# A new order for an mLSTM layer with a ReLU block: attention inputs first, all four decay blocks on TensorE

## The chip, the cores and the metric

One core of a Trainium2 chip. The metric is the device time of one execution in microseconds; the profile shows one execution, its span and what each engine did in it. Engines are named as in the profile: PE is TensorE (PEld its weight loads), DVE is VectorE, ACT is ScalarE, POOL is GpSimd, SP issues most transfers. A line such as L547 is a line of the kernel.

## The reference

Two stages. First a recurrent attention with exponential gates over 768 steps, for 4 batches of 8 heads of 40 elements; then a normalisation and a two-layer ReLU block (320 to 1280 to 320) on the result, added to it.

```python
m_new = np.maximum(f_gate[:, :, t] + m, i_gate[:, :, t])
f_stab = np.exp(f_gate[:, :, t] + m - m_new)
i_stab = np.exp(i_gate[:, :, t] - m_new)
C = f_stab[:, :, None, None] * C + i_stab[:, :, None, None] * np.einsum('bhd,bhe->bhde', vt, kt)
n = f_stab[:, :, None] * n + i_stab[:, :, None] * kt
h_tilde = np.einsum('bhde,bhe->bhd', C, qt)
y[:, :, t] = o * h_tilde / np.maximum(np.abs(np.einsum('bhd,bhd->bh', n, qt)[:, :, None]), 1.0)

xn = (x - mu) / np.sqrt(var + 1e-06) * g_ln
out = x + np.maximum(xn @ w_ch1, 0.0) @ w_ch2
```

All inputs are float32. The two weight matrices come as float64 bit patterns and are turned into float32 on the chip.

## The kernel before

The 768 steps are cut into 6 chunks of 128; a chunk and a batch make one of 24 **steps** (st = 4 * chunk + batch), and two steps a **pair** p of 256 rows for the ReLU block. Inside a chunk the recurrence is done as attention with a decay: a 128x128 block of weights per head, plus a carried state for all but the first chunk.

Each piece of work is a small function, and ORDER, a table of some 1180 words, calls them one after the other; `S.4@1@2` calls S for step 4 on PSUM banks 1 and 2. No scheduler changes the order: each engine's instructions run in the order of the table, and an engine that waits holds all that is behind it on its queue. SP's transfers and the few that ScalarE issues itself (gst, gse) stand in their engines' queues likewise. The framework gives each transfer one of eight completion counters in turn, over both queues; a transfer is issued only when the one that had its counter before has landed.

The pieces, with their lines:
- ld (L198) loads q and k of a step, tok (L203) the rows of k, v and the output gate of a pair, wl (L598) a raw weight block: block 0 is the rest of w_ch1, odd blocks are columns of w_ch1 (512 wide), even ones rows of w_ch2 (640 wide).
- gm, gg, gate, gu make the gate rows of a chunk (VectorE, from the second chunk on partly GpSimd); gst (L275) and gse (L283) write two of them to memory, from where G (L212) and eg (L223) read them back, broadcast over partitions. gta, gtr (L287) transpose gate columns, gca, gcr copy them, gr and gex are exponents.
- The decay block of a step: G loads it, sel (L320, GpSimd) masks it, ex (L331, ScalarE, 8 heads) takes the exponents. For steps below GP the block is made in PSUM instead by gx (L340, L346), ten matmuls, and ex reads it there.
- S (L363) multiplies k and q, P (L370, VectorE) applies the block, pv (L449) multiplies with v. km (L384, GpSimd) and kv (L415) update the state; qm (L376, GpSimd) and int (L400) read it. st (L434, ScalarE in the first chunk) stores the state, sig (L314, ScalarE) takes the output gate's tanh. n1, n2, n3 (VectorE) and nx, sq (ScalarE), np (GpSimd) normalise, T (L513, L514) transposes, xh and xl split the result into a high and a low part.
- m1 (L547) and hh, hl (L552, L559) are the first layer in column blocks f of 256, m2 (L574 to L576) the second, ob (L581) the sum, out (L588) the store.
- A weight block passes cA (L607, ScalarE), cB (L614, GpSimd), cT twice (L624, L628, VectorE), cH (L650, ScalarE, the high part) and cL (the low part: L679 on VectorE; for blocks 1 and 3 cI on TensorE and L676 on ScalarE). m1 and m2 need both parts, so each f waits for its blocks. cR copies part of block 0 to other partitions.
- fill (L726) are matmuls whose result nobody reads, 20 of them at the start.

Of the kernel before, what the change touches and what calls it, by code (L numbers as in the profile page):

```python
# [44 lines left out]
g0 ini id gin wl.2 wl.0 cst fill.513 fill.513 fill.496 fill.496 fill.496 fill.496 fill.256 fill.256 fill.256 fill.256  # L45
fill.320 fill.320 fill.320 fill.320 fill.257 fill.257 fill.257 fill.257 ld.1 ld.2 gm.0 wl.3 gg.0 ld.0 gate.0 gu.0
gst.0 gm.1 gg.1 cA.2 G.2 G.3 cB.2 gate.1 ld.3 gex.1 gst.1 tok.0 gx.1@0@1 cA.0 cB.0 tok.1 cT.2.0 wl.1 gse.1 ld.5 cT.2.1
gu.1 gta.0@2 gx.0@3@4 gr.0 gca.0 cT.0.0 ex.1.1 gtr.0@5 ex.1.0 S.1@2@6 g8 gm.2 ex.0.1 gta.1@1 fill.512 ld.4 gcr.0 P.1.1
gg.2 S.2@0@5 gr.1 cT.0.1 cA.3 gtr.1@4 fill.513 cH.2 cB.3 ex.0.0 fill.513 gca.1 P.1.0 cH.0 cT.3.0 S.0@1@6 cL.2 sel.2
fill.513 int.0@2@3 gcr.1 gate.2 P.0.0 gex.2 fill.513 gu.2 gst.2 P.0.1 ex.2.1 fill.512 fill.512 cT.3.1 gse.2 sel.3  # L50
gta.2@4 fill.512 ex.2.0 fill.512 gm.3 fill.512 S.3@1@6 cL.0 gg.3 ex.3.0 fill.513 cH.3 P.2.0 fill.512 cR.2 fill.512
gr.2 cR.0 P.2.1 cI.3@0 ex.3.1 eg.2 P.3.0 G.4 gca.2 gate.3 gtr.2@5 sig.0 km.1 pv.0 wl.4 P.3.1 cR.1 gst.3 gu.3 gcr.2
cL.3 int.1@4@5 pv.1 n1.0 gex.3 n2.0 gse.3 kv.1@1 km.0 gm.4 gta.3@6 n3.0 int.2@2@3 st.1 gg.4 kv.0@0 gr.3 n1.1 gtr.3@1
nx.0 gca.3 pv.2 n2.1 sq.0 gcr.3 n3.1 sig.1 int.3@4@5 pv.3 np.0 G.5 st.0 tok.2 cA.1 n1.2 T.0@6 km.3 wl.5 gate.4
fill.512 nx.1 fill.512 ld.6 n1.3 km.2 sq.1 n2.2 kv.3@1 cR.3 n2.3 ld.9 xh.0 T.1@0 cB.1 n3.2 gst.4 wl.9 kv.2@2 gex.4
n3.3 np.1 xh.1 S.5@3@4 nx.2 xl.1 gu.4 sq.2 fill.512 fill.512 nx.3 xl.0 fill.512 st.2 S.4@0@5 cT.1.0 sq.3 np.2 st.3
T.2@6 gm.5 gse.4 np.3 T.3@2 m1.0.1.0@1 xh.2 cT.1.1 xh.3 qm.5 xl.2 cH.1 wl.6 m1.0.1.1 xl.3 gta.4@6 gg.5 hh.0.1 gca.4
cI.1@2 gr.4 hl.0.1 gtr.4@6 m1.1.1.0@1 gcr.4 sel.4 cL.1 gate.5 gex.5 gst.5 int.5@6@7 cB.4 gse.5 m1.0.0.0@2 ex.4.0 sd.5
gu.5 m1.0.0.1 ex.4.1 P.4.0 m1.1.1.1 cA.4 sel.5 P.4.1 hh.0.0 cT.4.0 gta.5@0 m1.1.0.0@5 hh.1.1 qm.4 gca.5 ex.5.0 hl.0.0
m1.1.0.1 hl.1.1 ex.5.1 cT.4.1 m2.0.0.0@0 P.5.0 hh.1.0 wl.7 int.4@1@2 km.5 G.8 cH.4 P.5.1 pv.4 km.4 sig.2 hl.1.0 pv.5  # L60
sd.4 cL.4 m2.0.0.1@3 cA.5 cB.5 n1.5 n1.4 m2.1.0.1@4 cT.5.0 n2.5 m2.1.0.0@5 cT.5.1 m2.1.1.0 n2.4 cH.5 wl.8 n3.5 ld.7
m2.0.1.0 n3.4 nx.5 sq.5 cL.5 m2.1.1.1 nx.4 np.5 m2.0.1.1 sq.4 cB.9 cA.9 m1.1.2.0@6 np.4 cT.9.0 m1.1.2.1 cT.9.1
m1.0.2.0@7 cH.9 wl.10 cB.6 G.6 hh.1.2 ld.8 kv.4@1 cL.9 eg.3 cA.6 kv.5@2 m1.0.2.1 hl.1.2 tok.3 cA.7 cB.7 st.4 G.9
cT.6.0 m1.0.4.0@6 G.7 hh.0.2 G.11 st.5 ld.10 cT.6.1 m1.1.4.0@1 sel.8 hl.0.2 cH.6 m1.1.4.1 cT.7.0 ex.8.0 m1.0.4.1 cL.6
ex.8.1 cT.7.1 S.6@2@7 cB.8 cA.8 m2.0.2.1 cH.7 cT.8.0 m2.0.2.0 hh.0.4 cL.7 hh.1.4 m2.1.2.0 hl.0.4 m2.1.2.1 hl.1.4 cA.10
cB.10 cT.8.1 m1.0.3.0@6 cH.8 cT.10.0 m1.0.3.1 cL.8 sel.6 m1.1.3.0@1 hh.0.3 cT.10.1 ex.6.1 m1.1.3.1 hl.0.3 cH.10
m2.0.3.1 P.6.1 ex.6.0 cL.10 T.4@6 qm.7 T.5@7 m2.0.3.0 hh.1.3 P.6.0 xh.4 m2.0.4.1 hl.1.3 xh.5 qm.6 xl.4 m2.1.3.0 ob.0.1
m2.0.4.0 xl.5 out.0.1 sig.3 km.6 eg.4 m2.1.3.1 ob.0.0 km.7 ld.11 m1.2.0.0@2 out.0.0 tok.4 sel.9 m1.2.1.0@1 m1.2.0.1
ex.9.0 S.7@3@6 sel.7 ex.9.1 S.8@0@7 ex.7.0 m2.1.4.0 sel.11 P.8.0 hh.2.0 P.8.1 ex.7.1 m1.2.3.0@0 P.7.0 ex.11.1 m1.2.3.1
hl.2.0 ob.1.0 S.9@3@7 ex.11.0 P.7.1 m2.2.0.1@2 P.9.0 P.9.1 kv.7@5 kv.6@6 m1.2.4.0@3 m2.2.0.0@7 m2.1.4.1 m1.2.1.1  # L70
ob.1.1 hh.2.3 hl.2.3 m1.2.4.1 hh.2.1 km.9 sig.4 hl.2.1 m1.2.2.0@4 km.8 hh.2.4 m1.2.2.1 hl.2.4 m2.2.1.0 hh.2.2 hl.2.2
S.10@0@1 int.6@3@4 pv.6 sd.6 st.6 m2.2.1.1 n1.6 n2.6 m2.2.2.1 n3.6 m2.2.3.1 sq.6 nx.6 np.6 int.7@3@4 pv.7 sd.7 qm.8
st.7 m2.2.2.0 n1.7 n2.7 T.6@6 qm.9 n3.7 m2.2.3.0 xh.6 int.8@3@4 pv.8 xl.6 sq.7 kv.9@5 nx.7 sd.8 G.10 np.7 kv.8@6 n1.8
m2.2.4.0 ld.13 n2.8 tok.5 st.8 eg.5 n3.8 T.7@3 m2.2.4.1 xh.7 ob.2.0 sq.8 xl.7 S.11@4@6 out.2.0 nx.8 ld.15 np.8 ob.2.1
ld.12 m1.3.2.0@7 out.1.0 P.11.0 sel.10 G.13 P.11.1 m1.3.2.1 ex.10.0 m1.3.0.0@3 hh.3.2 P.10.0 T.8@2 m1.3.4.0@4 ex.10.1
hl.3.2 m1.3.0.1 xh.8 P.10.1 xl.8 m1.3.3.0@6 hh.3.0 sig.5 km.11 hl.3.0 m1.3.3.1 km.10 m1.3.1.0@0 hh.3.3 qm.11 hl.3.3
m1.3.1.1 m1.3.4.1 hh.3.1 hl.3.1 m2.3.0.0@7 m2.3.0.1@1 int.9@2@3 S.13@0@6 sd.9 qm.10 st.9 pv.9 m2.3.1.1 sel.13 ld.17
n1.9 eg.6 n2.9 m2.3.1.0 n3.9 ex.13.0 G.12 ld.14 m2.3.2.0 out.1.1 nx.9 P.13.0 out.2.1 m2.3.3.0 ex.13.1 T.9@5 sq.9
m2.3.2.1 P.13.1 xh.9 np.9 m2.3.3.1 xl.9 hh.3.4 int.11@2@3 hl.3.4 S.12@0@6 sd.11 qm.13 int.10@4@5 m2.3.4.1 sd.10 sel.12
# [5 lines left out]
xh.11 kv.13@2 ob.4.0 sq.12 S.15@3@5 st.12 out.4.0 nx.12 xl.11 np.12 G.16 S.16@1@4 G.15 tok.7 m2.4.3.1 out.3.0
m1.5.0.0@0 m1.5.0.1 m1.5.2.0@6 sel.16 hh.5.0 hl.5.0 m2.4.4.1 ex.16.0 m2.5.0.0@0 ob.4.1 sel.15 ex.16.1 P.16.0
m1.5.1.0@7 ex.15.0 P.16.1 m1.5.2.1 ex.15.1 m1.5.1.1 P.15.0 hh.5.2 m2.5.0.1@1 P.15.1 hh.5.1 km.15 hl.5.2 sig.7 T.12@4
km.14 m1.5.3.0@3 hl.5.1 xh.12 xl.12 m1.5.3.1 m2.5.1.0 hh.5.3 hl.5.3 m1.5.4.0@5 int.13@6@7 S.17@3@4 sd.13 qm.14 st.13
pv.13 kv.15@2 qm.15 n1.13 G.17 m1.5.4.1 n2.13 G.19 n3.13 m2.5.1.1 ld.19 hh.5.4 tok.8 nx.13 hl.5.4 m2.5.2.1 eg.8 sq.13
# [704 lines left out]
```

## Time and profile before

| | |
|---|---|
| median of 3 runs | 342.15 us (339.23 to 343.68) |
| the profiled execution | 344.09 us, its span 341.6 us |
| TensorE busy | 323.3 us (95%), 5182 matmuls |
| VectorE busy | 185.6 us (54%) |
| ScalarE busy | 156.7 us (46%) |
| GpSimd busy | 114.5 us (34%) |
| memory | 50.25 MB moved, mean 147 GB/s |

Busy time is the time in which an engine executes something; the shares are means over a start in which all engines and the transfers are in use at once, and a long later part in which TensorE is the only full one. A row of a timeline gives the start, the length, engine, line, what is written and read, the count, and in brackets how long the engine was idle before it and what released it.

### The profile page before, as it was taken

Reading aid. Unit: us, or ns where it says so; the run is one execution under the profiler, and the core shown is the slowest. Engines: PE = TensorE matmul, PEld = TensorE weight load, DVE = VectorE, ACT = ScalarE, POOL = GpSimd, SP = SyncE. Lnnn points to the kernel's source line nnn. Section 1 sums busy time; section 2 is a strip of 40 time slices with the busy share of each in tenths; the row PEclk is TensorE's granted clock in tenths of the full one; section 3 lists DMA queues with packets and bytes.
Section 4 is the critical chain, followed back from the end, with each engine's and each line's share of the span. In section 5 each row is a group of like instructions: output and inputs, shape, how many; then the busy total and the mean of one; then the engine's idle time right before and its main releaser. Section 6 shows DMA issues by size and latency. Waiting matters only on the chain.

```text
span 341.6 us, 11893 instructions
## 1 busy us (share of the span) xinstructions
PE 323.3 (95%) x5182; PEld 301.7 (88%) x5182; DVE 185.6 (54%) x429; ACT 156.7 (46%) x405; POOL 114.5 (34%) x163
## 2 busy tenths in 40 slices
...
GB/s 230 274 361 209 297 263 126 230 242 338 12 148 112 2 221 258 56 201 263 18 30 317 3 264 223 53 4 208 372 60 2 176 12 118 4 60 0 79 0 38
DMA packets 16287, 50.25 MB, mean 147 GB/s; under 512 B 2092, under 2 KB 5612, under 8 KB 16236
## 3 DMA queue, kind: packets, MB, share of 16 engines
...
q14 instruction: 11, 0.09, 0.1%
...
## 4 chain that ended last, share of the span: by engine, by line
PE 81%; DMA 14%; DVE 2%; ACT 1%; issue 1%; ACTq 1%; DVEq 0%
PE banks L547 30%; PE banks L574 11%; PE banks L576 10%; PE banks L575 10%; DMA qk<-in_qk_dram 10%; PE banks L363 5%; PE banks L449 5%; PE banks L400 3%; DMA gsc<-gc 2%; PE banks L415 2%; PE banks L513 2%; DMA w<-gsc 2%; PE banks L514 1%; DVE wt L628 1%; ACT w L331 1%
## 5 line engine op out<-in xcount | busy, mean ns | idle before, releaser
L575 PE MATMUL banks<-w2l,hh 128*128 128x320 f32 x240 | 74.7, 311 | 3.2 <-DVE w2l L679 2.9
L576 PE MATMUL banks<-w2h,hl 128*128 128x320 f32 x240 | 75.0, 313 | 2.9 <-DVE hl L559 2.9
L574 PE MATMUL banks<-w2h,hh 128*128 128x320 f32 x240 | 77.4, 322 | 0.0
L552 ACT ACTIVATE hh<-banks 128x512 fp32r<-128x512 f32 x60 | 35.0, 592 | 86.3 <-PE banks L547 73.5
L559 DVE SCALAR_TENSOR_TENSOR hl<-banks,hh 128x512 fp32r<-128x512 f32 x60 | 40.9, 688 | 61.5 <-ACT hh L552 61.4
L547 PE MATMUL banks<-xh,w1h 128*128 128x256 f32 x360 | 64.0, 286 | 0.7 <-DVE w L370 0.7
L547 PE MATMUL banks<-xh,w1l 128*128 128x256 f32 x360 | 62.3, 282 | 0.0
L331 ACT ACTIVATE w<-w,ar_sb 128x128 f32<-128x128 f32 x176 | 53.9, 389 | 16.2 <-POOL w L320 14.2
L547 PEld LDWEIGHTS banks<-xh,w1h 128*128 128x128 f32 x360 | 51.5, 188 | 1.9 <-DVE w L370 0.9
L547 PEld LDWEIGHTS banks<-xh,w1l 128*128 128x128 f32 x360 | 51.1, 188 | 0.0
L576 PEld LDWEIGHTS banks<-w2h,hl 128*128 128x128 f32 x240 | 45.7, 190 | 3.7 <-DVE hl L559 3.1
L547 PE MATMUL banks<-xl,w1h 128*128 128x256 f32 x240 | 48.0, 282 | 0.7 <-issue 0.7
L575 PEld LDWEIGHTS banks<-w2l,hh 128*128 128x128 f32 x240 | 45.8, 191 | 3.1 <-DVE w2l L679 3.1
L574 PEld LDWEIGHTS banks<-w2h,hh 128*128 128x128 f32 x240 | 45.8, 191 | 1.4 <-issue 0.7
L370 DVE TENSOR_TENSOR w<-banks,w 128x512 f32<-128x512 f32 x48 | 31.7, 684 | 17.0 <-ACT w L331 6.8
L376 POOL TENSOR_TENSOR qe<-qk,eg 104x512 f32<-104x512 f32 x20 | 27.4, 1378 | 35.3 <-PE banks L400 29.7
L547 PEld LDWEIGHTS banks<-xl,w1h 128*128 128x128 f32 x240 | 36.9, 188 | 0.8 <-issue 0.8
L501 POOL TENSOR_SCALAR rs<-rs 128x1 f32<-128x1 f32 x24 | 5.4, 227 | 87.9 <-ACT junk L495 87.8
L320 POOL TENSOR_SCALAR_AFFINE_SELECT w<-w 128x1024 f32<-128x1024 f32 x22 | 25.3, 1155 | 22.5 <-DMA w<-gsc 22.5
L384 POOL TENSOR_TENSOR kp<-tok,ar_sb 128x320 f32<-128x320 f32 x20 | 14.3, 731 | 38.5 <-PE banks L415 29.1
L581 DVE SCALAR_TENSOR_TENSOR y<-banks,rs,y 128x320 f32<-128x320 f32 x24 | 13.1, 550 | 26.0 <-PE banks L576 25.7
L363 PE MATMUL banks<-qk 40*64 40x128 f32 (+1 forms) x704 | 26.4, 275 | 0.0
...
## 6 DMA issues: line engine op xcount, KB each, us to landing
tok<-in_tok_dram SPq DMA_DIRECT2D x12, 968.0 KB
w<-gsc SPq DMA_DIRECT2D x22, 512.0 KB
...
wraw<-in_w1a_dram SPq DMA_DIRECT2D x5, 512.0 KB
...
```

The source lines that it names most:

```text
L320: nc.gpsimd.affine_select(out=w, in_=w, pattern=[[0, H], [1, C]], compare_op=ALU.is_ge, fill=NEG, base=0, channel_multiplier=-1)
L331: nc.scalar.activation(out=w[:, h], in_=ps[:, hh], func=AF.Exp, bias=ar_sb[:, c, 0, b * H + h:b * H + h + 1])
L363: nc.tensor.matmul(s_t[st, z][m, g], t[r, 1, g, m], t[r, 0, g], start=True, stop=True, skip_group_check=True)
L370: nc.vector.tensor_tensor(out=w, in0=s_t.pop((st, half)), in1=w, op=ALU.mult)
L376: nc.gpsimd.tensor_tensor(out=t, in0=qk_t[st][:, 0], in1=eg_t[p][:, j], op=ALU.mult)
L449: nc.tensor.matmul(Y[m, h], w[:, h, m], tok_t[p][:, j, h * VA:(h + 1) * VA], start=(c == 0), stop=(c == 0 or g == 3), skip_group_check=True,)
L547: nc.tensor.matmul(ps[:, i], a, x, start=(n == 0), stop=(n == len(ops) - 1))
L552: nc.scalar.activation(out=t, in_=h1_t[p, f], func=AF.Relu)
L559: nc.vector.scalar_tensor_tensor(out=l.rearrange("p a t -> p (a t)"), in0=ps.rearrange("p a t -> p (a t)"), scalar=0.0, in1=t.rearrange("p ...
L574: nc.tensor.matmul(ps, t[:, i, sl], w2h[:, ff], start=(ff == 0), stop=False)
L575: nc.tensor.matmul(ps, t[:, i, sl], w2l[:, ff], start=False, stop=False)
L576: nc.tensor.matmul(ps, l[:, i, sl], w2h[:, ff], start=False, stop=(ff == KF - 1))
```

## The change

ORDER is written anew, and GP goes from 2 to 4: the decay blocks of steps 2 and 3 are made by gx too. With that G.2, G.3, sel.2, sel.3 and gst.0 go, and gx.2 and gx.3 come; five float32 fills (fill.513) stand in the table instead of seven, the 13 fill.512 and the 16 others remain. All other pieces are the same ones in other places. km alternates its two buffers in the order of the calls, not by step. The variant "q" of CX that cA and cB now know isn't used, since CX is unchanged.

```diff
-GP = 2
+GP = 4
 NE = 4
 CX = "ppppppppppp"
@@ ORDER, its first words
-g0 ini id gin wl.2 wl.0 cst fill.513 fill.513 ...
+gin ini id g0 ld.0 ld.2 wl.0 fill.513 fill.513 ...
@@ km
+        kp_t[st] = kps[len(kp_t) % 2]
         kn = tok_t[p][:, j, VT:VT + DM].rearrange("p (h e) -> p h e", h=H)
         nc.gpsimd.tensor_tensor(
-            out=kps[st % 2][:, :DM].rearrange("p (h e) -> p h e", h=H), in0=kn,
+            out=kp_t[st][:, :DM].rearrange("p (h e) -> p h e", h=H), in0=kn,
@@ kv
-        kf = kps[st % 2]
+        kf = kp_t[st]
@@ cA
-        nc.scalar.activation(out=t.bitcast(F32), in_=hi.bitcast(F32), func=AF.Copy, scale=TINY)
+        if CX[n] == "q":
+            nc.gpsimd.tensor_scalar(out=t.bitcast(F32), in0=hi.bitcast(F32), scalar1=TINY, scalar2=None, op0=ALU.mult)
+        else:
+            nc.scalar.activation(out=t.bitcast(F32), in_=hi.bitcast(F32), func=AF.Copy, scale=TINY)
@@ cB
-        if CX[n] == "p":
+        if CX[n] in "pq":
```

The first twelve transfers on SP's queue, from the program's start, before (wraw is a raw weight block, qk the q and k of a step, w a broadcast gate row, tok a pair's rows):

```order
L187 DMA g0_sb_121<-in_gate0_dram 96x256
L191 DMA gin_122<-in_gates_dram 32x1280
L598 DMA wraw_155<-in_w2_dram 128x640
L598 DMA wraw_157<-in_w1r_dram 128x640
L194 DMA g_sb_104<-in_consts_dram 128x3
L198 DMA qk_178<-in_qk_dram 104x1024
L198 DMA qk_180<-in_qk_dram 104x1024
L598 DMA wraw_183<-in_w1a_dram 128x512
L198 DMA qk_189<-in_qk_dram 104x1024
L212 DMA w_202<-gsc_131 128x1024
L212 DMA w_204<-gsc_131 128x1024
L198 DMA qk_208<-in_qk_dram 104x1024
```

and now:

```order
L190 DMA gin_122<-in_gates_dram 32x1280
L186 DMA g0_sb_121<-in_gate0_dram 96x256
L197 DMA qk_155<-in_qk_dram 104x1024
L197 DMA qk_157<-in_qk_dram 104x1024
L598 DMA wraw_159<-in_w1r_dram 128x640
L193 DMA g_sb_104<-in_consts_dram 128x3
L598 DMA wraw_180<-in_w1a_dram 128x512
L197 DMA qk_182<-in_qk_dram 104x1024
L202 DMA tok_185<-in_tok_dram 128x1936
L598 DMA wraw_191<-in_w1a_dram 128x512
L202 DMA tok_194<-in_tok_dram 128x1936
L197 DMA qk_203<-in_qk_dram 104x1024
```

The q/k blocks of steps 0, 2 and 1, both tok blocks and the q/k block of step 3 have moved ahead, the first block of w_ch2 from the third place to the thirteenth, and the two w are gone.

ScalarE's first instructions, before (gsc and esc are the two written gate rows, w_214 and w_240 the decay blocks in PSUM, wt a weight block on its way):

```order
L275 DMA gsc_131<-gc0_127 32x128
L607 ACT_TABLE_LOAD
L607 ACTIVATE wt_200<-wraw_155 128x640
L279 ACTIVATE gg1_126<-gc1_128 32x128
L275 DMA gsc_131<-gc1_128 32x128
L607 ACTIVATE wt_225<-wraw_157 128x640
L283 DMA esc_132<-gg1_126 32x128
L309 ACTIVATE uu0_129<-uu0_129,gc0_127 96x128
L331 ACTIVATE w_214<-banks_99,ar_sb_110 128x128 x8
L331 ACTIVATE w_240<-banks_99,ar_sb_110 128x128 x4
L309 ACTIVATE uu1_130<-uu1_130,gc1_128 32x128
L607 ACTIVATE wt_299<-wraw_183 128x512
```

and now, behind the table load:

```order
L278 ACTIVATE gg1_126<-gc1_128 32x128
L308 ACTIVATE uu0_129<-uu0_129,gc0_127 96x128
L282 DMA esc_132<-gg1_126 32x128
L610 ACTIVATE wt_226<-wraw_159 128x640
L330 ACTIVATE w_207<-banks_99,ar_sb_110 128x128 x8
L330 ACTIVATE w_228<-banks_99,ar_sb_110 128x128 x4
L610 ACTIVATE wt_283<-wraw_180 128x512
L330 ACTIVATE w_228<-banks_99,ar_sb_110 128x128 x4
L330 ACTIVATE w_272<-banks_99,ar_sb_110 128x128 x4
L653 ACTIVATE w1h_111<-wt_226,g_sb_104 64x640 x2
L330 ACTIVATE w_309<-banks_99,ar_sb_110 128x128 x4
```

The exponents of four decay blocks follow each other, with the weight blocks 0 and 1 between them; the first gate row isn't written any more.

GpSimd at the two last weight blocks (w_ch2's, cB of blocks 8 and 10), before, with the decay selects, qm and km around them:

```order
L614 TENSOR_SCALAR wraw_970<-wraw_970 128x640
L614 TENSOR_SCALAR wraw_1043<-wraw_1043 128x640
L320 AFFINE_SELECT w_1046<-w_1046 128x1024
L376 TENSOR_TENSOR qe_1294<-qk_975,eg_1070 104x512
L376 TENSOR_TENSOR qe_1318<-qk_554,eg_1070 104x512
L384 TENSOR_TENSOR kp0_119<-tok_1101,ar_sb_110 128x320
L384 TENSOR_TENSOR kp1_120<-tok_1101,ar_sb_110 128x320
L320 AFFINE_SELECT w_1107<-w_1107 128x1024
L320 AFFINE_SELECT w_1118<-w_1118 128x1024
L320 AFFINE_SELECT w_1122<-w_1122 128x1024
```

and now:

```order
L617 TENSOR_SCALAR wraw_1077<-wraw_1077 128x640
L384 TENSOR_TENSOR kp0_119<-tok_1101,ar_sb_110 128x320
L384 TENSOR_TENSOR kp1_120<-tok_1101,ar_sb_110 128x320
L617 TENSOR_SCALAR wraw_1170<-wraw_1170 128x640
L384 TENSOR_TENSOR kp0_119<-tok_1190,ar_sb_110 128x320
L384 TENSOR_TENSOR kp1_120<-tok_1190,ar_sb_110 128x320
L375 TENSOR_TENSOR qe_1449<-qk_493,eg_1231 104x512
L375 TENSOR_TENSOR qe_1470<-qk_671,eg_1231 104x512
```

The selects have left this place, and the two qm stand behind the km of both pairs. VectorE at the same two blocks (wt_1186 and wt_1225 before, the low parts w2l; hl and P between them):

```order
L628 SCALAR_TENSOR_TENSOR wt_1186<-wraw_970,wt_1186 128x640
L624 SCALAR_TENSOR_TENSOR wt_1225<-wt_1225,wraw_1043 128x640
L679 SCALAR_TENSOR_TENSOR w2l_114<-wt_1186,w2h_113 128x640
L628 SCALAR_TENSOR_TENSOR wt_1225<-wraw_1043,wt_1225 128x640
L559 SCALAR_TENSOR_TENSOR hl_1274<-banks_99,hh_1259 128x512
L370 TENSOR_TENSOR w_1046<-banks_99,w_1046 128x512
L679 SCALAR_TENSOR_TENSOR w2l_114<-wt_1225,w2h_113 128x640
L370 TENSOR_TENSOR w_1046<-banks_99,w_1046 128x512
```

and now (wt_1301 and wt_1346):

```order
L682 SCALAR_TENSOR_TENSOR w2l_114<-wt_1188,w2h_113 128x640
L627 SCALAR_TENSOR_TENSOR wt_1301<-wt_1301,wraw_1077 128x640
L631 SCALAR_TENSOR_TENSOR wt_1301<-wraw_1077,wt_1301 128x640
L682 SCALAR_TENSOR_TENSOR w2l_114<-wt_1301,w2h_113 128x640
L559 SCALAR_TENSOR_TENSOR hl_1348<-banks_99,hh_1336 128x512
L627 SCALAR_TENSOR_TENSOR wt_1346<-wt_1346,wraw_1170 128x640
L559 SCALAR_TENSOR_TENSOR hl_1391<-banks_99,hh_1382 128x512
L631 SCALAR_TENSOR_TENSOR wt_1346<-wraw_1170,wt_1346 128x640
L682 SCALAR_TENSOR_TENSOR w2l_114<-wt_1346,w2h_113 128x640
```

Behind each cB on GpSimd the two cT and the low part follow on VectorE as before; both P have moved away from between them.

## Rows read from the trace of the kernel before

**Rows 1.** busy us by stretch: us, PE, PEld, DVE, ACT, POOL; clock, DMA share, GB/s

```profile
0.00:8.10 8.10, 6.38 (x20) 3.92 (x21) 3.39 (x15) 2.18 (x3) 4.20 (x18) 1.00 0.72 226
8.10:45.00 36.90, 31.49 (x408) 22.06 (x406) 26.21 (x66) 23.74 (x70) 24.06 (x38) 0.91 0.94 291
45.00:95.00 50.00, 43.00 (x554) 40.63 (x552) 40.84 (x66) 32.88 (x81) 29.20 (x32) 0.93 0.63 190
95.00:338.20 243.20, 242.40 (x4208) 235.13 (x4206) 114.58 (x282) 97.92 (x254) 57.01 (x77) 1.00 0.37 115
```

**Rows 2.** TensorE's waits, whole run (us in total, times, longest)

```profile
PE banks L575 <- DVE w2l L679: 2.9, 1, 2.9
PE banks L576 <- DVE hl L559: 2.9, 1, 2.9
PE banks L287 <- ACT uu L309: 2.2, 1, 2.2
PE banks L415 <- ACT w1l L676: 2.0, 1, 2.0
```

**Rows 3.** stretches after TensorE's waits, columns as in rows 1

```profile
33.80:37.00 3.20, 3.17 (x53) 2.95 (x55) 1.46 (x7) 3.20 (x9) 2.06 (x4) 0.50 0.82 230
92.00:94.70 2.70, 2.70 (x13) 2.70 (x12) 1.28 (x3) 2.48 (x7) 0.00 (x0) 0.50 0.01 3
```

**Rows 4.** ScalarE's timeline (start us, us), then two pieces of the chain of waits

```profile
25.24 0.72 ACT L314 ACTIVATE tok<-tok 128x640 f32<-128x640 f32 x1
29.85 0.31 ACTq L275 DMA_DIRECT2D gsc<-gc  x1
30.20 0.60 ACT L676 ACTIVATE w1l<-banks 128x512 fp32r<-128x512 f32 x1 [4.25 <-DVE y L471]
32.82 0.32 ACTq L283 DMA_DIRECT2D esc<-gg  x1
...
4.84 6.59 DMA gsc<-gc
16.14 16.30 DMA qk<-in_qk_dram
```

**Rows 5.** timeline of GpSimd, then of VectorE, around the last weight blocks

```profile
79.73 3.82 POOL L376 TENSOR_TENSOR qe<-qk,eg 104x512 f32<-104x512 f32 x2 [3.73 <-DMA eg<-esc]
83.50 1.41 POOL L384 TENSOR_TENSOR kp<-tok,ar_sb 128x320 f32<-128x320 f32 x2
84.86 3.77 POOL L320 TENSOR_SCALAR_AFFINE_SELECT w<-w 128x1024 f32<-128x1024 f32 x3
...
79.74 0.82 DVE L628 SCALAR_TENSOR_TENSOR wt<-wraw,wt 128x640 int32<-128x640 int32 x1
82.32 4.32 DVE L679 SCALAR_TENSOR_TENSOR w2l<-wt,w2h 128x640 fp32r<-128x640 f32 x1
86.56 2.75 DVE L628 SCALAR_TENSOR_TENSOR wt<-wraw,wt 128x640 int32<-128x640 int32 x1
```

**Rows 6.** two weight lines' VectorE instructions: ns least/median/most

```profile
L624 DVE SCALAR_TENSOR_TENSOR wt<-wt,wraw x11: 677/825/1923, 8.5 to 80.5; 128x640 int32<-128x640 int32 x6, 128x512 int32<-128x512 int32 x5
...
L679 DVE SCALAR_TENSOR_TENSOR w2l<-wt,w2h x5: 809/818/4316, 16.9 to 90.4; 128x640 fp32r<-128x640 f32 x5
```

**Rows 7.** TensorE's timeline: one decay block, four float32 fill matmuls

```profile
9.92 0.59 PE L340 MATMUL banks<-mk_bf,id_bf 128*128 128x512 bf16 x2
10.44 1.16 PE L346 MATMUL banks<-gc,id_sb 32*128 32x128 f32 x16
...
17.52 1.98 PE L726 MATMUL banks<-id_sb 128*128 128x512 f32 x4
```

**Rows 8.** ScalarE's exponents from PSUM until 45 us (xcount, busy us, mean ns)

```profile
L331 ACT ACTIVATE w<-banks,ar_sb 128x128 f32<-128x128 f32 x16 | 4.3, 385 | 0.3 <-DVE ar_sb L299 0.3
```

**Rows 9.** page, transfers issued: count, size of each

```profile
tok<-in_tok_dram SPq DMA_DIRECT2D x12, 968.0 KB
w<-gsc SPq DMA_DIRECT2D x22, 512.0 KB
```

149 lines of the change are left out of this document (74 added, 75 removed).

## The prediction

> **What bounds the kernel now.** I read the stretches first, then TensorE's waits, then the granted clock, then the queues behind the waits. By stretch [rows 1], TensorE is busy 242.4 of the 243.2 us from 95 to 338: there is nothing to win there except TensorE work itself. All that can be won lies before 95. From 8.1 to 45 (the first m1 starts at 45) it works 31.5 of 36.9 us, from 45 to 95 it works 43.0 of 50.0: 5.4 + 7.0 = 12.4 us idle. Four waits make 10.0 of the 12.4 [rows 2].
>
> Each pair of waits is followed by a stretch at the lower of the two clock levels (1.2 instead of 2.4 GHz): 0.50 from 33.8 to 37 and 0.50 from 92 to 94.7 [rows 3]; the timeline shows the same level from about 33.5 to 40.3 and from about 90 to 95. The first is full of small matmuls that lose less than half: I put it at 2.7 us. The second is about 4.9 us of wide matmuls, half of it lost: 2.4 us. So 12.4 + 2.7 + 2.4 = 17.5 us is the most that better feeding can give back.
>
> Why TensorE waits, first pair: ScalarE's queue is in order, and stands in front of two small transfers that it issues itself. After the tanh at 25.24 nothing starts until the gate row's transfer is let go at 29.85; the eviction of the low half of a weight block (w1l) follows at 30.20, and TensorE had waited 2.0 us for it. The next such transfer goes at 32.82, and 2.2 us of TensorE wait for the exponent behind it [rows 2, 4]. The chain of waits names what was late: a q/k transfer issued at 16.14 that landed 16.30 us later, behind all that was already queued; and SP's own queue stood 6.59 us, from 4.84 to 11.43, before its ninth transfer [rows 4].
>
> Second pair: VectorE is 100% busy from 80 to 90, but with two instructions stretched. The low half of a weight block (w2l) takes 4.32 us, the next weight step (L628) 2.75, while GpSimd runs instruction after instruction until 88.6 [rows 5]. Undisturbed the first takes 0.81 at the least [rows 6], and the second took 0.82 at 79.74 [rows 5]. So about 5.4 us of VectorE is lost to GpSimd's burst, and the 5.8 us of TensorE's waits at 83.8 to 90 are that.
>
> **What the change does to each part.**
>
> TensorE work. Two more decay blocks (gx.2, gx.3): a mask pair and 16 row matmuls each, 9.92 to 11.60, so 1.6 us each, 3.2 together [rows 7]. Two float32 fills fewer: four matmuls take 1.98 with the last one's tail, two to a fill, so about 0.95 each, 1.9 together [rows 7]. Net +1.3 us, on the path, since the later stretch has no slack.
>
> What goes with it: two broadcast loads of 512 KB, their two GpSimd selects, and the first gate row's transfer gst.0, the one that held SP for 6.59 us. ScalarE's exponents of those steps now read PSUM at 4.3 / 16 = 0.27 us each [rows 8].
>
> Transfers. With the sizes in [rows 9] (and, by their shapes, 416 KB for a q/k block, 160 and 96 KB for the gate rows, 512 and 640 KB for the two kinds of weight block), everything up to and including tok.1 was 6.7 MB and is now 5.1 MB. At the rates of [rows 1], 226 GB/s to 8.1 us and 291 after, tok.1 landed by 25 us and now lands by 19.5; wl.2, the last of that batch, by 23. pv.2, the first reader of tok.1, cannot come before about 26 by TensorE's own work. So the inputs of four steps are there in time, and where a ninth transfer must wait for one of the eight before it, that one has less in front of it. Later weights (wl.5, 9, 7, 6, 8, 10) wait behind tok.2, which needs pv.1; I put tok.2's issue at 34, its landing at 40, wl.5's at 47, against a use near 60. I cost this at nothing; the cover is some 9 us, and what is later than that counts one for one.
>
> TensorE up to the first m1. Before: 31.5 us of work, of which 2.7 was slow clock, so 28.8. Now +1.3, and work that is taken ahead of the first m1: S.6 (1.0), cI.1 (1.0) and three gate transposes (0.3). 28.8 + 1.3 + 2.3 = 32.4, so the first m1 cannot start before 8.1 + 32.4 = 40.5.
>
> ScalarE up to the first m1 [rows 1, 8]. Before it was busy 2.2 + 23.7 = 25.9 us until 45. Now come 16 more exponents (4.3 us; ex.4 and ex.6 take the place of ex.2 and ex.3 in SBUF), one eviction more (0.6), one more gate exponent (0.4), a fourth xh (0.5), cH.1 for cH.2 (0.2): 31.9, less the 1.3 of the table load, which now lies ahead of the first work. From about 8.4 (the first gate exponent stood at 7.98, and g0 is now issued second, 0.45 later) that is 39.0. So ScalarE has as little room as TensorE: any wait of one passes to the other. Its idle time from 8.1 to 45 was 36.9 - 23.7 = 13.2 us, of which the two transfer holds were 6.5; so 6.7 were ordinary waits on the other engines. From below the new loss is nothing, from above 6.7 plus another 2.7 of slow clock. I take 3.5, half of the ordinary waits without slow clock, since ScalarE's first reason to wait (its transposes) has work to fill it. First m1 at 44.0.
>
> VectorE and GpSimd after the first m1. The weight blocks' steps read two SBUF tensors. From the first m1 to the last w2l there are 9 steps of 640 columns at 0.82, 6 of 512 at 0.68 [rows 6], and eight low halves at about 0.81: 18 us. GpSimd was busy 29.2 us from 45 to 95 [rows 1]; in the same stretch it now has three selects (3.8) and a qe pair (3.8) less [rows 5], and otherwise the same work: about 22 us as it ran, its own stretches included. The stretch is 38.7 us of TensorE work. The places changed: before, qe, qe, kp, kp and three selects stood next to the last two blocks; now only four kp and one weight step do, and the qe pair follows after. The 9 us burst is gone from that place. From below the remaining loss is 0, from above the old 7.0 + 2.4 = 9.4. I take 2.5, about two stretched steps of the smaller kind (1.92 where the median is 0.83 [rows 6], so 1.1 each) that reach TensorE.
>
> The Trainium skill, SBUF — State Buffer, "Who interferes with whom", says that the pair of ports shared by VectorE and GpSimd is an exclusive lock, taken for a whole instruction by whoever comes first, and that a VectorE instruction with two SBUF inputs needs it against a GpSimd one that reads SBUF. The trace agrees on who is stretched [rows 5], but 4.32 us spans more than one GpSimd instruction, which the rule alone would not give. By the rule taken strictly the two loads add up, 18 + 22 = 40 us in 38.7, 1.3 over, which would put the time 1.2 below mine; by the rows one stretched step alone cost 3.5.
>
> The sum, on the profiled execution (344.09 us, span 341.6): -17.5 recovered, +1.3 work, +3.5 and +2.5 new waits: -10.2, so 333.9. That execution is 1.9 above the median of the three (342.15). On the median it gives 332, which is the forecast.
>
> **Rivals.**
> - The burst returns. 18 us of VectorE and 22 of GpSimd share 38.7; one late transfer (as eg for the qe pair) bunches GpSimd's work again. For: the burst before began with a late eg [rows 5]. Against: the qe pair now stands after the last block. It costs the old 5.8 us plus 2.4 of clock, in place of my 2.5: 332 + 5.7 = 338. The Trainium skill's lock rule (SBUF — State Buffer, the section named above) speaks for this one too.
> - ScalarE bounds the start. It has 30.6 us to do in 32; if its ordinary waits stay at 6.7 and the slow clock at 2.7, the start loses 9.4 in place of 3.5: 338. Both rivals together: 344, no change.
> - Slower: ScalarE's queue is held once more. gse.3 needs ld.4's transfer to have landed, and SP issues ld.4 behind G.4, which needs the gate row gst.1 (issued about 20.6) to have landed. If gst.1 takes 6.6 us and ld.4 then 16.3 as its like did [rows 4], it lands at 43.5. ScalarE would stand from about 31: 12.5 us and some 3 of slow clock, 347.5. It decides from a hold of 10 us. Against: in front of ld.4 there is then less than 1 MB, not the 3 MB of that time (7.2 MB issued by 16.14, 4.2 moved at the rates of [rows 1]), so I expect it by about 32.
>
> **Numbers.** Forecast case, 326 to 335: 0.63. One of the first two rivals, 335 to 341: 0.23. Both, 341 to 349: 0.09. Held queue or more, beyond: 0.05. About 2% (6.8 us) is what a measurement of this kernel can tell from no change, so faster means below 335.3, slower above 349. Faster 0.64, same 0.31, slower 0.05. The lower end is no new wait at all (342.15 - 17.5 + 1.3 = 326), the upper end one rival and a little more: 326 to 340. The forecast's own range is 326 to 335.
>
> **What would show it.** First m1 (L547) at 44, not 45, with S.6 done. No ScalarE idle beside a gate row's transfer of over 1 us. SP's ninth transfer out by 5 us. No w2l step over 2 us. TensorE at full clock from 8 on. TensorE idle before 95 about 5 us instead of 12.4, and the stretch to the end as full as now. I am wrong if the first m1 comes after 47, if VectorE steps of 3 us and more return, or if new waits appear after 95.

## The result and the profile after

The changed kernel takes 327.7 us (median of four: 327.34 to 330.63) against 342.9 for the kernel before beside it: ratio 0.961, 95% interval 0.9505 to 0.9715. It is faster, by 15 us, where 10 were forecast. The ratios, here and in the experiments, are of the faster executions alone: one that lies over 1.5% above the fastest of its kernel is left out of them. The profiled execution took 327.43 us, its span is 325.6; TensorE is busy 98% of it. Against the profiled execution of before (344.09) that is 16.7 us, where the sum said 10.2.

Stretches of the changed kernel, cut at its own first m1 (columns: stretch, its length, busy time and count of each engine, granted clock, share of the DMA engines, GB/s), to be laid beside [rows 1]:

```profile
8.10:41.20 33.10, 32.48 (x477) 23.46 (x475) 26.91 (x71) 28.48 (x87) 22.81 (x39) 1.00 0.90 282
41.20:95.00 53.80, 53.47 (x845) 50.90 (x844) 44.72 (x85) 34.05 (x83) 29.97 (x35) 1.00 0.83 247
95.00:322.00 227.00, 226.68 (x3875) 220.54 (x3874) 103.88 (x259) 92.14 (x236) 55.13 (x73) 1.00 0.37 109
```

From 8.1 to 95 TensorE is idle 0.6 + 0.3 us, where it was 12.4, and the clock is at its full level throughout, where two stretches stood at half [rows 3]. After 95 TensorE is as full as it was (idle 0.3 of 227.0 us, 0.8 of 243.2 before). So nearly all of it was gained where the prediction looked, and no wait took the place of the four of [rows 2]. TensorE's waits in the whole execution (us in total, times, longest; the first is the start of the program):

```profile
PE banks L729 <- POOL id_sb L698: 1.7, 1, 1.7
PE banks L513 <- ACT xn L489: 0.3, 1, 0.3
PE banks L339 <- ACT w L330: 0.3, 1, 0.3
PE banks L547 <- DVE xh L531: 0.3, 1, 0.3
```

The timelines of TensorE, ScalarE and SP at the places of [rows 2, 4]: the S of step 6 lies ahead of the first m1, the first m1 is at 41.18 instead of 44.98, ScalarE's gate transfers (ACTq) go without a hold, and SP's ninth transfer, the first tok, goes at 4.93 and the third (tok.2) at 34.50.

```profile
38.33 1.10 PE L362 MATMUL banks<-qk 40*64 40x128 f32 x32
...
41.18 0.50 PE L547 MATMUL banks<-xh,w1h 128*128 128x256 f32 x2
```

```profile
30.78 0.31 ACTq L282 DMA_DIRECT2D esc<-gg  x1
...
37.19 0.40 ACT L308 ACTIVATE uu<-uu,gc 32x128 f32<-32x128 f32 x1 [1.64 <-PE banks L286]
```

```profile
4.93 0.39 SPq L202 DMA_DIRECT2D tok<-in_tok_dram  x1
...
34.50 0.35 SPq L202 DMA_DIRECT2D tok<-in_tok_dram  x1
```

The weight stage, to be laid beside [rows 5]: first VectorE and GpSimd at the first two w2 blocks, then GpSimd and VectorE at the last one.

```profile
43.69 0.82 DVE L627 SCALAR_TENSOR_TENSOR wt<-wt,wraw 128x640 int32<-128x640 int32 x1
...
43.93 2.43 POOL L384 TENSOR_TENSOR kp<-tok,ar_sb 128x320 f32<-128x320 f32 x2
...
49.42 1.55 DVE L682 SCALAR_TENSOR_TENSOR w2l<-wt,w2h 128x640 fp32r<-128x640 f32 x2
...
50.35 1.57 POOL L319 TENSOR_SCALAR_AFFINE_SELECT w<-w 128x1024 f32<-128x1024 f32 x1 [1.05 <-DMA w<-gsc]
...
81.93 3.13 POOL L375 TENSOR_TENSOR qe<-qk,eg 104x512 f32<-104x512 f32 x2
...
82.19 1.72 DVE L682 SCALAR_TENSOR_TENSOR w2l<-wt,w2h 128x640 fp32r<-128x640 f32 x1 [0.81 <-ACT w2h L653]
```

No w2l takes more than 1.72 us, where one took 4.32. The sharing is still there, but now GpSimd's instructions are the longer ones (kp 2.43, qe 3.13 for two), and it has pauses to make up for it. The last w2l still runs beside the qe pair.

### The profile page after: what moved, and what is told of

It reads as the page before. It is cut to its first block, busy times and chain, and to the rows that moved or that the text cites. A ratio compares the mean times of both kernels' runs of the same rounds, so it can differ in the third digit from the quotient of the medians.

```text
span 325.6 us, 11933 instructions
## 1 busy us (share of the span) xinstructions
PE 319.3 (98%) x5214; PEld 298.9 (92%) x5214; DVE 179.1 (55%) x429; ACT 155.9 (48%) x405; POOL 111.4 (34%) x161
## 4 chain that ended last, share of the span: by engine, by line
PE 96%; ACT 2%; DVE 1%; issue 0%; POOL 0%; DVEq 0%; POOLq 0%
PE banks L547 36%; PE banks L574 12%; PE banks L575 11%; PE banks L576 11%; PE banks L362 7%; PE banks L449 5%; PE banks L400 3%; PE banks L729 3%; PE banks L415 3%; PE banks L513 2%; PE banks L345 1%; ACT w L330 1%; PE banks L514 1%; PE banks L339 1%; PE banks L667 1%; PE banks L286 1%
## 5 line engine op out<-in xcount | busy, mean ns | idle before, releaser
L576 PE MATMUL banks<-w2h,hl 128*128 128x320 f32 x240 | 74.1, 309 | 0.0
L330 ACT ACTIVATE w<-w,ar_sb 128x128 f32<-128x128 f32 x160 | 49.0, 390 | 9.6 <-POOL w L319 9.5
L576 PEld LDWEIGHTS banks<-w2h,hl 128*128 128x128 f32 x240 | 45.0, 188 | 0.0
L375 POOL TENSOR_TENSOR qe<-qk,eg 104x512 f32<-104x512 f32 x20 | 26.3, 1328 | 26.1 <-PE banks L400 16.5
L319 POOL TENSOR_SCALAR_AFFINE_SELECT w<-w 128x1024 f32<-128x1024 f32 x20 | 23.0, 1149 | 33.9 <-DMA w<-gsc 33.8
L384 POOL TENSOR_TENSOR kp<-tok,ar_sb 128x320 f32<-128x320 f32 x20 | 18.2, 928 | 23.0 <-PE banks L415 14.2
L362 PEld LDWEIGHTS banks<-qk 40*64 40x64 f32 (+1 forms) x704 | 21.6, 138 | 2.9 <-issue 1.4
```

Of the source, the lines that this page charges most:

```text
L319: nc.gpsimd.affine_select(out=w, in_=w, pattern=[[0, H], [1, C]], compare_op=ALU.is_ge, fill=NEG, base=0, channel_multiplier=-1)
L330: nc.scalar.activation(out=w[:, h], in_=ps[:, hh], func=AF.Exp, bias=ar_sb[:, c, 0, b * H + h:b * H + h + 1])
L362: nc.tensor.matmul(s_t[st, z][m, g], t[r, 1, g, m], t[r, 0, g], start=True, stop=True, skip_group_check=True)
L375: nc.gpsimd.tensor_tensor(out=t, in0=qk_t[st][:, 0], in1=eg_t[p][:, j], op=ALU.mult)
L384: nc.gpsimd.tensor_tensor(out=kp_t[st][:, :DM].rearrange("p (h e) -> p h e", h=H), in0=kn, in1=ar_sb[:, c, 1, b * H:(b + 1) * H].unsqueeze ...
L576: nc.tensor.matmul(ps, l[:, i, sl], w2h[:, ff], start=False, stop=(ff == KF - 1))
```

## The experiments

The medians of before lie between 341.2 and 342.9 us in the sets of runs below, so each ratio is to the before that ran beside it. A difference to the changed kernel is to its 327.7, which was taken beside another before, and is uncertain by those 2 us.

**1. The burst alone.** The kernel before, with GpSimd's work beside the last blocks held back; behind the hold two of the selects now come first.

```
+    def hold():
+        nc.gpsimd.tensor_copy(out=dg_sb[0:1, 0, 0:1], in_=w2l[0:1, 9, DM - 1:DM].bitcast(F32))
-  ... cL.10 T.4@6 qm.7 ... qm.6 ... km.6 ... km.7 ... sel.9 ... sel.7 ... sel.11
+  ... cL.10 hold sel.9 sel.7 km.6 km.7 qm.7 qm.6 sel.11 T.4@6 ...
```

> The kernel before, with GpSimd's last burst of the weight stage held back: a one-element copy on GpSimd that reads the low half of the last weight block stands in front of two kp, two qe and three selects, so they start only when VectorE is through with the blocks. Nothing else changes. Theory (waits): the low half steps (w2l) stay under 2 us, TensorE's two waits of 2.9 us near 84 to 90 and the half clock behind them (2.4 us) go; 5.8 + 2.4 less up to 1.5 for work that now comes later: 5.5 to 8 us faster. Rival (the same GpSimd work has to share the memory with VectorE somewhere): the stretched steps and a wait of TensorE come a little later, gain under 2 us.

334.05 us against 341.24, ratio 0.9785 (0.9743 to 0.9827): 7.2 us faster. VectorE's two w2l of the last blocks, and GpSimd behind the hold:

```profile
81.64 0.83 DVE L678 SCALAR_TENSOR_TENSOR w2l<-wt,w2h 128x640 fp32r<-128x640 f32 x1
...
84.37 0.82 DVE L678 SCALAR_TENSOR_TENSOR w2l<-wt,w2h 128x640 fp32r<-128x640 f32 x1
```

```profile
85.33 0.18 POOL L723 COPY dg_sb<-w2l 1x1 f32<-1x1 f32 x1 [9.03 <-DVE w2l L678]
...
87.57 1.40 POOL L383 TENSOR_TENSOR kp<-tok,ar_sb 128x320 f32<-128x320 f32 x2
88.93 2.54 POOL L375 TENSOR_TENSOR qe<-qk,eg 104x512 f32<-104x512 f32 x2
```

The theory holds: from 80 to 95 TensorE has no wait, the clock stays up, and kp and qe take their undisturbed times (0.70 and 1.27 each) 4 to 9 us later without anybody waiting. The second pair of waits with its clock was 8.2 us in the prediction; 7.2 came back.

**2. ScalarE's hold alone.** The kernel before, with the two transfers that held ScalarE issued by SP.

```
     def gst(c):
-        nc.scalar.dma_start(out=gsc[c], in_=gc[c % 2][0:BH])
+        (nc.sync if c == 3 else nc.scalar).dma_start(out=gsc[c], in_=gc[c % 2][0:BH])
     (gse likewise)
```

> The kernel before, with the two gate row transfers of chunk 3 (gst.3, gse.3) issued by SP instead of ScalarE, at the same places of the table; they still wait for the same transfers, but ScalarE does not. Theory (ScalarE is held): no idle of over 1 us on ScalarE between 25 and 33, TensorE's waits for w1l (2.0) and for the gate exponent uu (2.2) go with the half clock from 33.8 to about 40 (2.7): first m1 at 38.5 to 41 instead of 45, whole time 4 to 7 us faster. Rival (ScalarE's own work is the bound of the start, the hold only stands in a pause it would have anyway): first m1 not before 43.5, gain under 2 us.

341.35 us against 341.24, ratio 0.9966 (0.9929 to 1.0002): no difference that can be told. The first m1 comes at 43.10 instead of 44.98, far from the 38.5 to 41 expected, and TensorE has other waits in front of it: for the copied gate columns (L303) 2.1 and for GpSimd's uu 1.5. It is idle as long as in the kernel before, 5.4 us up to the first m1 and 7.1 from there to 95, so the theory falls.

**3. Both.**

> The kernel before with both edits: GpSimd's burst held back until the last weight block is through, and the two gate row transfers of chunk 3 issued by SP. Theory (two separate losses): the gains add up, 10 to 14.5 us faster, about 328 to 332, so near the changed kernel without a new order of the rest. Rival (one of them hides the other, because work that comes earlier meets the next late transfer): under 8 us faster.

334.17 us, ratio 0.9798 (0.9765 to 0.9830): what the first edit gives alone. The gains don't add up, and the profile shows why. TensorE's waits before the first m1 (us in total, times, longest), and ScalarE's timeline at that place:

```profile
PE banks L362 <- ACT xn L488: 2.8, 1, 2.8
PE banks L362 <- DMA qk<-in_qk_dram: 2.5, 2, 1.3
```

```profile
29.72 0.31 ACT L433 ACTIVATE state<-banks 104x164 f32<-104x164 f32 x1 [1.78 <-PE banks L414]
...
38.09 0.31 ACTq L274 DMA_DIRECT2D gsc<-gc  x1
38.45 0.31 ACT L278 ACTIVATE gg<-gc 32x128 f32<-32x128 f32 x1 [4.26 <-DMA eg<-esc]
```

The state's copy comes at 29.72 instead of 33.19 [rows 4], so the hold is gone. Then ScalarE runs into the next gate transfer, which waits for eg until 38.09, and S behind it waits for ScalarE; S had waited for q/k blocks before that, ahead of 17.57 and of 23.36. The hold by itself didn't set the time: ScalarE, freed of it, stood 4.26 us at the next late transfer. That the transfers as a whole were late is my reading of this; experiment 6 tests it on the changed kernel.

**4. The two decay blocks alone.** The kernel before with GP 4 in the old order.

```
-GP = 2
+GP = 4
-  ... gst.0 ... G.2 G.3 ... S.2@0@5 ... ex.0.0 ... cL.2 sel.2 ... int.0@2@3 ... ex.2.1 ... sel.3 ... ex.2.0 ... ex.3.0 ... ex.3.1
+  ... gx.2@0@5 ... ex.0.0 ex.2.1 ex.2.0 ... S.2@0@5 ... cL.2 gx.3@2@3 ex.3.1 ex.3.0 ... km.1 int.0@2@3 ...
```

> The kernel before, with the decay blocks of steps 2 and 3 on TensorE (GP 4; the two broadcast loads, the two selects and gst.0 go; gx.2 and gx.3 stand near the places where ex read the loaded blocks; S.2 and int.0 moved a little for their banks); all the rest in the old order. Theory (waits): TensorE has 3.2 us more to do, SP's queue opens at about 5 instead of 11.4, so the transfers behind it land some us earlier and ScalarE is held some 3 to 6 us less; the collision of the last weight blocks stays. Together between 3 us slower and 3 us faster. Rival (the blocks on TensorE, and 1 MB less to move, are what the new order gains by): 8 us faster or more.

Three executions took 350.6, 352.3 and 352.4 us, three others 361.2 to 366.8. Ratio 1.0321 (1.0284 to 1.0358), of the first three: 11 us slower, outside both expectations. The blocks are no gain by themselves, and in an order that wasn't made for them a loss. Which wait makes the 11 us stays open: the profile is of the 361.2, so not of one of these three. In it the first m1 comes at 50.20, 5.2 us later than in the kernel before, which points at the start but doesn't show it for the others.

**5. Without the later fills.** The changed kernel without the 16 fills that stand behind those of the start (18 fills, 20 matmuls).

> The changed kernel without the 16 fills that stand behind the first 20 (about 7 us of TensorE before the first m1). Theory (in the new order TensorE's own work sets the first m1, as in the forecast's floor of 40.5 us, in which these fills are counted): the first m1 comes 3 to 7 us earlier and the time falls by as much, 321 to 325. First rival (the fills lie in pauses that stay): the pauses show as TensorE idle, first m1 within 1.5 us of where it is, time within 1.5 us. Second rival (the clock falls to its lower level in the pauses): granted clock 0.5 in some stretch between 12 and 45, 2 to 5 us slower.

Ratio 0.972 (0.9632 to 0.9808) to before. The six times lie apart: 328.8, 328.8, 332.3, 334.7, 334.9, 335.7; the ratio is of the first three. The profile is of the 334.7 and tells of the longer executions only. The stretch to its first m1 (at 41.79, 0.6 later than with fills), and the one behind:

```profile
8.10:41.80 33.70, 30.05 (x466) 23.06 (x464) 26.72 (x71) 29.08 (x87) 23.41 (x39) 0.95 0.90 277
41.80:60.00 18.20, 15.25 (x145) 14.32 (x144) 17.12 (x19) 11.66 (x31) 12.51 (x16) 0.78 1.00 267
```

The theory falls: none of the six is faster than the changed kernel's 327.7. In this profile both rivals show: 3.7 us of idle stand where the fills were, and the clock falls (0.50 from 38.6 to 44.6). The two executions at 328.8 lie within the first rival's 1.5 us; what sets them apart from the others no profile shows. TensorE's work didn't set the first m1 though my floor came out right; the fills in that floor are filling. What comes behind 41.8 is experiment 8's subject: a wait of 2.9 us for w2l.

**6. Weights first.** The changed kernel, with three loads ahead of the two tok.

```
-gin ini id g0 ld.0 ld.2 wl.0 ... cst wl.1 ld.1 gm.0 tok.0 gg.0 wl.3 gate.0 tok.1 ... wl.2 ... ld.4
+gin ini id g0 wl.2 ld.0 ld.2 wl.0 ... cst wl.1 wl.3 ld.1 ld.4 gm.0 tok.0 gg.0 gate.0 tok.1 ...
```

> The changed kernel, with only the order of the first transfers put nearer to the old one: two weight blocks (wl.2 before ld.0, wl.3 behind wl.1) and the fifth q/k block (ld.4 behind ld.1) go ahead of the rows of k, v and gate (tok.0, tok.1); 1.5 MB more ahead of tok.1. All else is unchanged. Theory (the order of the transfers is what shortens the start): tok.0 lands 3 to 5 us later and tok.1 5 us later, km and pv wait for them; the first m1 comes 3 to 6 us later, with TensorE idle and some half clock in front of it; 330.5 to 335. Rival (the order matters little, the old losses came from the gate row transfers on ScalarE's queue): within 1.5 us of the changed kernel.

343.46 us, ratio 1.0102 (1.0035 to 1.017): the whole gain is gone and more, 16 us against the changed kernel. GpSimd's first kp, the stretch up to the first m1 (at 49.82), and TensorE's longest wait behind it:

```profile
23.09 1.40 POOL L384 TENSOR_TENSOR kp<-tok,ar_sb 128x320 f32<-128x320 f32 x2 [4.58 <-DMA tok<-in_tok_dram]
```

```profile
8.10:49.80 41.70, 38.90 (x479) 28.04 (x477) 26.69 (x70) 28.65 (x87) 22.72 (x39) 0.84 0.81 238
```

```profile
PE banks L575 <- DVE w2l L682: 4.0, 1, 4.0
```

kp comes at 23.09 where the changed kernel has it at 17.03, and TensorE runs at half clock for all of 20 to 30: the first m1 is 8.6 us later, more by the clock than by idle time (TensorE works 38.90 of the 41.70 us). To that come the 4.0 us of w2l. More than expected, and on the theory's side: the order in which the first 5 MB come is what this start hangs on. The first m1 is also 4.8 us later than in the kernel before, so this isn't the old start put back but a worse one.

**7. Two of the four decay blocks loaded again.** The changed kernel with GP 2.

```
-GP = 4
+GP = 2
-  ... gate.0 tok.1 ... gx.2@1@2 ... ex.2.1 gg.2 S.2@5@6 ex.2.0 ... g8 ... ex.1.1 ... gx.3@0@2 ... km.1 ... P.0.0
+  ... gate.0 gst.0 tok.1 G.2 G.3 ... g8 sel.2 ... ex.1.1 ex.2.1 ex.2.0 ... S.2@0@2 ... km.1 sel.3 ... P.0.0 P.2.1 P.2.0
```

> The changed kernel, with the decay blocks of steps 2 and 3 loaded and masked again as before (GP 2; gst.0, G.2, G.3, sel.2, sel.3 come back behind tok.1; S.2, ex.2 and P.2 moved behind those of step 1 for it). Theory (the blocks on TensorE are a price of 3.2 us that pays by freeing the transfers and GpSimd): TensorE has 3.2 us less to do, but 1 MB more is moved in a start in which the transfers are busy 0.9 of the time, and SP waits for gst.0: first m1 0 to 4 us later than 41.2, 327 to 332. Rival (the new order alone does it, the blocks on TensorE only cost): 2 to 3.5 us faster, 324 to 326.

342.89 us, ratio 1.0107 (1.0055 to 1.0159): 15 us lost, where 0 to 4 were expected and the rival said a gain. GpSimd waits for the loaded block with the first kp behind it, ScalarE for GpSimd, and TensorE for a kp:

```profile
21.29 1.10 POOL L319 TENSOR_SCALAR_AFFINE_SELECT w<-w 128x1024 f32<-128x1024 f32 x1 [4.31 <-DMA w<-gsc]
...
22.42 2.45 ACT L330 ACTIVATE w<-w,ar_sb 128x128 f32<-128x128 f32 x8 [7.59 <-POOL w L319]
```

```profile
PE banks L415 <- POOL kp L384: 4.4, 1, 4.4
```

The first m1 comes at 48.59, 7.4 later, and behind it stands the same 4.0 us for w2l. So in this order the price of 3.2 us of TensorE buys more than twice that in the start. A part of it may be the places I chose: sel.2 ahead of kp, and ex.2 where ScalarE's queue stands 7.59 us for it. The run doesn't separate that from the load itself.

**8. The burst put back.** The changed kernel, with ten products on GpSimd beside the last two blocks.

```
+    def bm():   # 104x256, two inputs in SBUF
+        nc.gpsimd.tensor_tensor(out=dg_sb[:104]..., in0=w1h[:104, 0, 0:256]..., in1=w1h[:104, 1, 0:256]..., op=ALU.mult)
-  ... cL.8 cB.10 cA.10 ...
+  ... cL.8 cB.10 bm bm bm bm bm bm bm bm bm bm cA.10 ...
```

> The changed kernel, with ten products on GpSimd (two inputs of 104x256 in SBUF, result not read) put in behind the last cB, so that GpSimd runs without a pause beside the last two weight blocks, some 7 us, as before the change. Theory (a GpSimd that runs instruction after instruction starves VectorE's two-input steps): a step of the last blocks takes over 3 us, TensorE waits 3 to 6 us before 90 and loses clock behind it: 4 to 8 us slower, 332 to 336. Rival (the old waits came from those blocks being late, not from GpSimd): no step over 2 us, within 1.5 us of the changed kernel.

333.01 us, ratio 0.9814 (0.9752 to 0.9876): 5 us slower than the changed kernel, as the theory wants, but not for its reason. Beside the products, which lie at 81 to 92, no VectorE step of the weight blocks takes over 1.39 us. In the profile, which is of the longest of the six (335.4), the largest loss stands at the first two w2 blocks, before the products begin; for the qe behind them TensorE waits 1.0 us. The rows of that place:

```profile
43.88 2.18 DVE L627 SCALAR_TENSOR_TENSOR wt<-wt,wraw 128x640 int32<-128x640 int32 x1
...
43.97 1.40 POOL L384 TENSOR_TENSOR kp<-tok,ar_sb 128x320 f32<-128x320 f32 x2
...
51.16 1.08 POOL L319 TENSOR_SCALAR_AFFINE_SELECT w<-w 128x1024 f32<-128x1024 f32 x1
...
51.32 5.25 DVE L682 SCALAR_TENSOR_TENSOR w2l<-wt,w2h 128x640 fp32r<-128x640 f32 x2
...
52.22 2.48 POOL L375 TENSOR_TENSOR qe<-qk,eg 104x512 f32<-104x512 f32 x2
...
55.44 0.63 PE L575 MATMUL banks<-w2l,hh 128*128 128x320 f32 x1 [3.67 <-DVE w2l L682]
```

Compare the rows of the changed kernel at this place. There VectorE's L627 got through (0.82) and the kp pair took 2.43; here the kp pair has its undisturbed 1.40 and L627 takes 2.18. By the starts L627 is ahead both times, by 0.24 and by 0.09 us; who came first is read from the lengths. VectorE is then later, and so is the gate it owes to GpSimd; the select, which in the changed kernel still waits for its transfer until the w2l are nearly through, now starts just ahead of them, and select and two qe keep w2l out: 5.25 us for two steps that took 1.55. TensorE waits 3.67 us, with half clock until 58. The profiles of experiments 5, 6 and 7 show the same (kp 1.40, L627 3.2 to 3.3, w2l pair 5.24 or 5.25).

**9, 10, 11. That place by itself.** The changed kernel again (9); with a hold of the kind of experiment 1 in front of sel.5, reading the second w2l (10); and that together with the ten products (11).

> The changed kernel once more, unaltered, for its own spread. In the four runs before this one, all that differ from it in something else (no fills, weights first, two gx, burst at the end), TensorE waited 2.9 to 4.0 us for a low half (w2l) between 50 and 60, beside a select and two qe of GpSimd; in the changed kernel's own profile VectorE was through with w2l 0.2 us before that select began. Theory (a matter of a few tenths of a us): most runs at 327 to 329, with the odd one 3 to 5 us above. Rival (the four were hit for reasons of their own): all within 327 to 331.

> The changed kernel, with a one-element copy on GpSimd in front of sel.5 that reads the end of the second w2l, so that sel.5 and the two qe behind it start only when VectorE has made both low halves of the first two w2 blocks. Nothing else changes. Theory: sel.5 starts about 1 us later than now, nobody waits for it, the two w2l take 1.6 to 2 us together in every run; 326 to 328.5 and no run above 329.5. Rival (the select, the qe and what ScalarE does with them are late then): 1 to 4 us slower.

> The changed kernel with both: sel.5 held behind the second w2l, and the ten GpSimd products beside the last two weight blocks of the run before (there 333.0, with two w2l of 5.25 us together at 51, long before the products, and no VectorE step over 1.4 us beside them). Theory (that loss was made at 51 and the products beside the last blocks cost only their own delay of kp and qe, about 1 us): the wait for w2l at 50 to 60 is gone, 328 to 329.5. Rival (the products at the end cost the 5 us): 332 to 334 again.

The changed kernel: 326.65 to 330.68, median 327.44, ratio 0.9647 (0.9584 to 0.9711). None of its ten times reaches 331, and its second profile shows the same order at this place as the first (L627 0.82, w2l pair 1.55). So the rival fits as well as my "odd one above"; why the four were hit each time and this one is not, when they differ elsewhere, I can't say.

With the hold: 329.59, ratio 0.9695 (0.963 to 0.976), no gain, rather 2 us more, as its rival has it. Its profile shows no large wait to explain them, only small ones (idle 1.4 us after 110). The hold does its work, though. GpSimd's kp came first here too, and still w2l is free:

```profile
43.77 2.18 DVE L626 SCALAR_TENSOR_TENSOR wt<-wt,wraw 128x640 int32<-128x640 int32 x1
...
50.32 1.55 DVE L681 SCALAR_TENSOR_TENSOR w2l<-wt,w2h 128x640 fp32r<-128x640 f32 x2
```

With hold and products: 333.66, ratio 0.9817 (0.9761 to 0.9873). The wait for w2l is gone and the time isn't better than experiment 8's: the products put kp and qe off by 7 to 10 us, and now TensorE waits for qe, with a granted clock of 0.90 from 85 to 95. At the first two w2 blocks VectorE's L627 got through here, so that the place may have been free without the hold:

```profile
44.27 0.83 DVE L627 SCALAR_TENSOR_TENSOR wt<-wt,wraw 128x640 int32<-128x640 int32 x1
...
44.37 2.57 POOL L384 TENSOR_TENSOR kp<-tok,ar_sb 128x320 f32<-128x320 f32 x2
```

```profile
PE banks L400 <- POOL qe L375: 2.2, 1, 2.2
```

So a full GpSimd at the last blocks does cost 4 us against experiment 10, as the rival has it, but through the late qe, not through stretched VectorE steps. The losses at the two places don't add up: with a wait of 3.7 us for w2l the one for qe was 1.0, without it 2.2 and some clock. How experiment 8's 5 us divide between the two these runs don't show.

**12. Longer products.** As 11, with six products of 104x512.

> As the run before (sel.5 held behind the second w2l, products on GpSimd beside the last two weight blocks), but six products of 104x512 instead of ten of 104x256 (the result, which nobody reads, is written as bf16). With the short ones no VectorE step of the last two blocks took over 1.4 us, where the kernel before shows 4.32 beside qe, kp and selects. Theory A (a two-input step of VectorE waits for the GpSimd instruction that is under way and comes next): no step over 0.82 + 1.3 = 2.1 us, several near 2. Theory B (instructions of GpSimd that follow each other without a gap keep VectorE out for several of them, if they are long): a step of 3 us or more, and a wait of TensorE for it. In both the kp and qe behind the products come late, as with the short ones: 332 to 336.

331.64 us, ratio 0.9686 (0.9597 to 0.9775), a little under the 332 to 336 expected. Theory A holds for these products: VectorE's longest step beside them is 1.80, and it is GpSimd that seems stretched (six in 10.89, 1.8 each, where an undisturbed qe of 104x512 takes 1.27).

```profile
76.53 10.89 POOL L731 TENSOR_TENSOR dg_sb<-w1h 104x512 bf16<-104x512 f32 x6
...
77.15 1.80 DVE L631 SCALAR_TENSOR_TENSOR wt<-wraw,wt 128x640 int32<-128x640 int32 x1
```

So among these products size doesn't decide whether VectorE gets its turn. The products all write one tile, while kp, qe and selects each write another; whether that is what leaves VectorE a gap wasn't tried and stays open.

## Why the prediction was right, and where it was not

**The forecast case and its sign: right.** 327.7 lies in the forecast's own range of 326 to 335, near its lower end, which was named as "no new wait at all". The mechanism held in what was recovered and failed in what was to be lost again: the two terms for new waits, 6.0 us together, came out at 0.9.

**17.5 us to be recovered: right.** Idle of 12.4 became 0.9, both stretches at half clock are gone. Experiment 1 confirms the second half by itself: 7.2 of 8.2.

**Work +1.3, floor 40.5: right in size.** First m1 at 41.18, with S.6 and cI.1 ahead of it. TensorE is busy 319.3 us in all, 4.0 less than before; the sum makes that 2.7 + 2.4 - 1.3 = 3.8. But the floor isn't what bounds the start: without 16 fills the first m1 is no earlier in the profile (41.79), and no execution takes less than 328.8 (experiment 5).

**New waits in the start, +3.5: the term that failed.** 0.6 was measured. I took half of ScalarE's old pauses for a loss of TensorE. ScalarE still has 3.7 us of pauses from 9.03 to 41.2, but TensorE works in them, on pieces and fills that were moved there. ScalarE's own work in that time was 28.5 us, where I had 30.6. The cause I gave for the old waits was wrong as well, or not enough: with ScalarE's queue freed of the two transfers the time stays as it was (experiments 2 and 3). What the new order repairs is, by the runs, the sequence of the transfers (experiment 6) together with what the decay blocks free (experiment 7, with the places left open there): undoing either loses the whole gain (4.0 us of it by the wait for w2l between 50 and 65), and the blocks in the old order cost 11 us (experiment 4). My sum took blocks and transfers for separate items.

**New waits in the weight stage, +2.5: failed in kind.** 0.3 was measured. The value was a middle between 0 and 9.4, but the place has two outcomes: nothing, as here, or 2.9 to 4.0 us of TensorE and half clock behind it (experiments 5 to 8). Without a hold it goes with which of kp and L627 is stretched; that this decides it isn't shown. In the forecast this is the rival "the burst returns", with 0.23 together with the second. It came in neither profile of the changed kernel, and in the experiments not at the last blocks where I looked for it but at the first two of w2. The forecast gave no reason why that place should stay free, so that it did was luck. The loads were off too: from the first m1 to the last w2l GpSimd was busy 26.7 us, not 22, in a stretch of 42.7 us, not 38.7, and the qe pair ran beside the last w2l, not behind it.

With 0.6 and 0.3 in place of 3.5 and 2.5 the sum is 15.3, of 16.7 measured. Of the rest 0.5 is idle after 95 that is gone (0.8 before [rows 1], 0.3 now), and 0.7 lies outside the span (344.09 - 341.6 = 2.5 before, 327.43 - 325.6 = 1.8 now); 0.2 I can't place.

**Late weights at nothing: right.** tok.2 goes out at 34.50 (34 forecast), and late weight blocks cost GpSimd pauses of 0.55 and 1.40 us, TensorE none.

**The held queue: rightly small.** gse.3 goes at 30.78 without a hold; ld.4, which it needs, was forecast to land by about 32.

**A rule on the ports.** The Trainium skill, SBUF — State Buffer, "Who interferes with whom", says "Issue order, not op shape, decides who blocks." The rows of kp and L627 fit it in that the same two shapes come out both ways, 0.82 and 2.43 or 2.18 and 1.40, but they don't test it: L627's record starts first both times. That a step waits for one GpSimd instruction is too little for the 2.18, which spans both kp (0.70 each), and for the 5.25 us, during which a select and two qe ran.
